# A first slot taken whole, two pairs' exponentials set by set, cheaper means, and a new order: an attention and MLP kernel on one core

## The chip, the cores and the metric

The kernel runs on one core of one Trainium2 chip. The metric is the device time of one execution in microseconds, and lower is better. Times of before: the median of three runs is 711.76 us (711.76 to 712.01).

## What is computed

The reference chains three parts over 2304 tokens of 512 features: an attention with masks, a gated MLP behind an RMS norm, and a second MLP whose activation is a softmax times its own input, with a layer norm behind it.

```python
# attention: B, H, S, D = 4, 8, 576, 64; 4 heads plain window 32, 4 heads dilated by 4
scores = scale * np.matmul(q, k.transpose(0, 1, 3, 2))
scores = np.where(masks[None, :, :, :], scores, -1000000000.0)
scores = scores - np.max(scores, axis=-1, keepdims=True)
attn = np.exp(scores)
attn = attn / (np.sum(attn, axis=-1, keepdims=True) + 1e-09)
out = np.matmul(attn, v)
# MLP: d_model 512, d_ff 1536
rms = np.sqrt(np.mean(x * x, axis=-1, keepdims=True) + 1e-06)
xn = x / rms * rms_g
g = xn @ w_gate
silu = g * (1.0 / (1.0 + np.exp(-g)))
x = silu * (xn @ w_val) @ w_out
# second MLP: d_ff 1024
h = x @ w_in
e = np.exp(h - h_max)
solu = h * e / (np.sum(e, axis=-1, keepdims=True) + 1e-09)
ln = (solu - mu) / np.sqrt(var + 1e-06) * g_ln
out = ln @ w_out
```

The weights arrive in 64-bit floating point, and the kernel makes 32-bit words of them itself.

## The kernel before

**Tiling.** The tokens are cut into nine pieces of 256 (`PIECES`). Pieces 0 and 1 are the early ones: their attention is done by `pair`, with two pairs of heads (t, 0) and (t, 1) each, at the start, while the inputs are still being loaded. Pieces 2 to 8 are done by `attention` later, in between the products of the MLP. The MLP works on parts of one or two pieces (`PARTS`): pieces 0 and 1 are part 0, with 512 columns of tokens. Its hidden dimension is cut into twelve slots f of 128. One slot has a gate product `g`, a value product `vp` (each against four blocks of 128 of the features), then tanh on ScalarE (`u`), the rest of the silu on VectorE (`u<-u,g`), the product with `vp` (`u<-u,vp`), and `y`, which is summed over all slots in four banks. Every product is done as three fp32r matmuls: high with high, low with high and high with low (L952 to L954), so each operand has a high part (a cast on ScalarE, `xh`, `uh`, `w`) and a low part (the rest, on VectorE or GpSimd, `xl`, `uh<-u,uh`, `w<-wf,w`).

**Weights.** `prepare` brings in a slot's three blocks, 0 for the gate, 1 for the values, 2 for y: `fetch` (a load on SyncE's queue of 512 KB, `raw<-w`), `shifted` (ScalarE, on the upper words), `parts` (VectorE, a right shift, L391), `joined` (VectorE, L395, `wf<-raw`), then high and low.

**Norm.** `rms` takes for the early pieces the mean by small `ms<-ones,sq` matmuls, a root on GpSimd (`r`), a diagonal matrix (`rd<-ident,r`, two of 128x128, VectorE, L858), and a `spread` matmul (`rs<-rd,ones`, L863), which puts it on all partitions. For the later pieces the mean comes from one fp32 matmul of 256 columns against `ones` (`ms<-sq,ones`, L827).

**Slot 0.** For part 0 the first slot is done in two halves, piece 0 and piece 1 (`HALVES = 1` and the first two rows of `VIRTUAL`): each half has a gate and a value product of 256 columns, a tanh, a silu, a product and a y of its own.

**Order.** Nothing in the code fixes the order of an engine's instructions by hand. Each piece of work is a step of `Plan`: a name, its cost by engine, the steps that it needs, the buffers that it takes (one bank is named `g`, two are named `vp` and `a`, and so on), and a due time. `order` takes step by step what can start first, and of those that can, the one due first. The table `NUDGE` shifts the due times of single steps, `ENGINE` forces an engine, `PACE` says from which slot on a later attention may begin. So a change to these tables moves instructions on all engines, and each engine then runs its list strictly in that order. Where the plan foresees a gap of TensorE ahead of 75 us (`FILL`), `fill` puts in matmuls on a constant `seed` whose result is overwritten. They are written into the bank that the next step uses:

```python
    def fill(x, add=False):
        while filling[0] > 0:
            filling[0] -= 1
            nc.tensor.matmul(x, (nothing if add else seed)[:, 0:1].to_broadcast([P, P]),
                             seed.to_broadcast([P, x.shape[1]]), start=not add, stop=not add)
```

The third block of work, the joint part for two later parts and the second MLP, is not touched but for its order and its plan costs.

Of the kernel before, what the change touches and what calls it, by code (L numbers as in the profile page):

```python
# [7 lines left out]
F32 = mybir.dt.float32  # L8
# [12 lines left out]
P = 128  # L21
# [4 lines left out]
TP = 256  # L26
# [18 lines left out]
def groups_of(piece):  # L45
# [30 lines left out]
    else:  # L76
# [7 lines left out]
        for at, bt in ((128, b), (192, b2)):  # L84
# [12 lines left out]
HALVES = 1  # L97
# [5 lines left out]
SINGLE = 7  # L103
# [85 lines left out]
class Plan:  # L189
# [20 lines left out]
    def order(self):  # L210
# [32 lines left out]
        while ready:  # L243
# [13 lines left out]
            if e == "p" and free["d"] > start:  # L257
                free["d"] += 0.45 * cost
# [27 lines left out]
def tile_attention_glu_solu(ctx: ExitStack, tc: tile.TileContext, qk_d, v_d, w1_d, win2_d, wout2_d,  # L286
# [24 lines left out]
    ones = const.tile([P, P], F32, name="ones")  # L311
    mhalf = const.tile([P, 4], F32, name="mhalf")
# [45 lines left out]
    def prepare(stage, f, cuts, srcs, scales, dues, needs=(), lead=((1, 0), "joined", 0)):  # L358
# [104 lines left out]
    def pair(t, m, due):  # L463
# [29 lines left out]
        def scores(e):  # L493
            x = new_bank(sp, [P, 8, 64], "sp")
            fill(x.rearrange("p s k -> p (s k)"))
            n = g["mask"]
# [28 lines left out]
        def exps(e):  # L525
            nc.scalar.activation(T[s_], T[sp], AF.Exp, scale=0.125)
# [1329 lines left out]
    for v in range(len(VIRTUAL)):  # L1856
        mlp(v, 1000 * (v + 1))
# [99 lines left out]
```

## Time and profile before

| | before |
|---|---|
| median of three runs | 711.76 us (711.76 to 712.01) |
| the profiled execution | 712.27 us |
| its span | 710.2 us |
| TensorE busy | 702.3 us, 99% |
| VectorE busy | 509.4 us, 72% |
| ScalarE busy | 358.9 us, 51% |
| GpSimd busy | 135.5 us, 19% |
| mean rate of the transfers | 137 GB/s |

The span runs from the first to the last instruction of the profiled execution; the rest of its time lies around it. Engines: PE is TensorE, DVE VectorE, ACT ScalarE, POOL GpSimd, SP SyncE, which issues the loads here. Matmuls are pipelined: the duration of one is longer than the step from one to the next. What a stretch can gain depends on what TensorE waits for there, not on how busy another engine is on average.

### The profile page before, as it was taken

Reading aid. Unit: us, or ns where it says so; the run is one execution under the profiler, and the core shown is the slowest. Engines: PE = TensorE matmul, PEld = TensorE weight load, DVE = VectorE, ACT = ScalarE, POOL = GpSimd, SP = SyncE. Lnnn points to the kernel's source line nnn. Section 1 sums busy time; section 2 is a strip of 40 time slices with the busy share of each in tenths; the row PEclk is TensorE's granted clock in tenths of the full one; section 3 lists DMA queues with packets and bytes.
Section 4 is the critical chain, followed back from the end, with each engine's and each line's share of the span. In section 5 each row is a group of like instructions: output and inputs, shape, how many; then the busy total and the mean of one; then the engine's idle time right before and its main releaser. Section 6 shows DMA issues by size and latency. Waiting matters only on the chain.

```text
span 710.2 us, 11738 instructions
## 1 busy us (share of the span) xinstructions
PE 702.3 (99%) x4533; PEld 593.3 (84%) x4533; DVE 509.4 (72%) x932; ACT 358.9 (51%) x769; POOL 135.5 (19%) x166
## 2 busy tenths in 40 slices
PE   8999999999999999999999999999999999999998
PEld 6788888899998888888888888888888888888887
DVE  5899899679585986668966766689677677665552
ACT  2976854344535554516655554355375555543440
POOL 0322432250506121110000000014044311010110
PEclk9999999999999999999999999999999999999999
DMA  9999433154368764403321112947032111000001
GB/s 336 401 407 354 133 101 118 64 185 141 134 225 293 276 206 141 141 7 125 123 72 37 52 60 97 344 139 220 1 119 75 60 60 45 30 16 30 30 30 45
DMA packets 42424, 97.21 MB, mean 137 GB/s; under 512 B 3841, under 2 KB 14081, under 8 KB 42369
## 3 DMA queue, kind: packets, MB, share of 16 engines
q1 hardware_dynamic: 40640, 93.33, 37.9%
q10 hardware_dynamic: 1728, 3.15, 1.2%
q8 instruction: 35, 0.57, 0.3%
q14 instruction: 21, 0.16, 0.1%
HBM read 72.87 MB, written 23.59 MB: 136 GB/s over the span
## 4 chain that ended last, share of the span: by engine, by line
PE 93%; DMA 5%; ACT 1%; DVE 1%; SPq 0%; issue 0%; ACTq 0%
PE y L952 7%; PE ca L1292 7%; PE y L954 7%; PE y L953 7%; PE o L1689 5%; PE o L1688 5%; PE o L1687 5%; PE g L952 4%; PE vp L952 4%; PE g L953 4%; PE g L954 4%; PE vp L954 4%; PE vp L953 4%; DMA raw<-w 3%; PE cd L1292 2%; PE cb L1292 2%
## 5 line engine op out<-in xcount | busy, mean ns | idle before, releaser
L342 POOL TENSOR_TENSOR w<-wf,w 128x512 fp32r<-128x512 f32 (+1 forms) x15 | 25.1, 1673 | 203.9 <-ACT w L333 203.9
L1687 PE MATMUL o<-w,lt 128*128 128x512 f32 (+1 forms) x152 | 58.9, 388 | 0.0
L1689 PE MATMUL o<-w,lt 128*128 128x512 f32 (+1 forms) x152 | 57.6, 379 | 0.0
L1688 PE MATMUL o<-w,lt 128*128 128x512 f32 (+1 forms) x152 | 57.5, 379 | 0.0
L952 PE MATMUL y<-uh,w 128*128 128x512 f32 (+1 forms) x148 | 53.2, 359 | 0.0
L954 PE MATMUL y<-uh,w 128*128 128x512 f32 (+1 forms) x148 | 51.7, 349 | 0.0
L953 PE MATMUL y<-uh,w 128*128 128x512 f32 (+1 forms) x148 | 51.7, 349 | 0.0
L660 ACT ACTIVATE s<-s,nm 128x64 f32<-128x64 f32 x120 | 40.1, 337 | 18.6 <-DVE nm L655 18.6
L333 ACT CAST w<-wf 128x512 fp32r<-128x512 f32 (+1 forms) x40 | 28.3, 728 | 25.5 <-DVE wf L395 11.5
L952 PE MATMUL g<-xh,w 128*128 128x512 f32 (+1 forms) x104 | 40.4, 389 | 0.0
L333 ACT CAST uh<-u 128x512 fp32r<-128x512 f32 (+1 forms) x37 | 19.9, 537 | 38.3 <-DVE u L996 37.7
L953 PE MATMUL g<-xl,w 128*128 128x512 f32 (+1 forms) x104 | 39.0, 375 | 0.2 <-DVE xl L342 0.2
L952 PE MATMUL vp<-xh,w 128*128 128x512 f32 (+1 forms) x100 | 39.0, 390 | 0.0
L954 PE MATMUL g<-xh,w 128*128 128x512 f32 (+1 forms) x104 | 38.9, 374 | 0.0
L954 PE MATMUL vp<-xh,w 128*128 128x512 f32 (+1 forms) x100 | 38.2, 382 | 0.0
L953 PE MATMUL vp<-xl,w 128*128 128x512 f32 (+1 forms) x100 | 38.1, 381 | 0.0
L805 POOL TENSOR_TENSOR sq<-x 128x256 f32<-128x256 f32 x28 | 17.8, 647 | 105.7 <-DVE x L337 61.6
L1655 POOL TENSOR_SCALAR st<-st 128x1 f32<-128x1 f32 x18 | 8.7, 484 | 140.5 <-ACT sq L1646 140.3
L992 DVE SCALAR_TENSOR_TENSOR u<-u,g 128x512 f32<-128x512 f32 (+1 forms) x37 | 21.5, 582 | 18.3 <-ACT u L986 18.3
L986 ACT ACTIVATE u<-g 128x512 f32<-128x512 f32 (+1 forms) x37 | 19.0, 514 | 27.9 <-PE g L954 27.2
L1689 PEld LDWEIGHTS o<-w,lt 128*128 128x128 f32 x152 | 28.6, 188 | 5.3
L342 DVE TENSOR_TENSOR lt<-tp,lt 128x512 fp32r<-128x512 f32 x36 | 23.2, 684 | 13.6 <-ACT lt L333 13.6
(290 smaller groups left out, 2056.5 us busy)
## 6 DMA issues: line engine op xcount, KB each, us to landing
raw<-w SPq DMA_DIRECT2D x36, 512.0 KB, 9.1
es<-ec SPq DMA_DIRECT2D x12, 512.0 KB, 3.1
sc<-es SPq DMA_DIRECT2D x12, 512.0 KB, 3.4
qk<-qk SPq DMA_DIRECT2D x7, 800.0 KB, 5.5
vt<-v SPq DMA_DIRECT2D x10, 512.0 KB, 5.6
wo<-w SPq DMA_DIRECT2D x9, 512.0 KB, 7.6
wst<-wo SPq DMA_DIRECT2D x9, 512.0 KB, 3.7
yT<-yo SPq DMA_DIRECT2D x16, 256.0 KB, 3.1
```

The source lines that it names most:

```text
L333: nc.scalar.copy(dst, src) if scale is None else nc.scalar.mul(dst, src, scale)
L342: ENG[e].tensor_tensor(dst, a, b, ALU.subtract)
L660: nc.scalar.activation(T[s_][:, i], T[s_][:, i], AF.Exp, bias=st["nm"][:, i:i + 1], accum_out=sm[:, i:i + 1])
L952: nc.tensor.matmul(acc, wh, xh, start=first, stop=False)
L953: nc.tensor.matmul(acc, wh, xl, start=False, stop=False)
L954: nc.tensor.matmul(acc, wl, xh, start=False, stop=last)
L986: return lambda e: nc.scalar.activation(new(up, ("u", v, f), [P, 512])[:, 0:n], T["g", v, f], AF.Tanh, scale=0.5)
L992: return lambda e: nc.vector.scalar_tensor_tensor(out=u_of(f), in0=u_of(f), scalar=1.0, in1=T["g", v, f], op0=ALU.add, op1=ALU.mult)
L1292: nc.tensor.matmul(acc(x), w, y, start=not more and j == 0 and n == 0, stop=j == 1 and n == 2, skip_group_check=True)
L1687: nc.tensor.matmul(o, lt[:, 0, k], w[:, 0], start=(k == 0), stop=False)
L1688: nc.tensor.matmul(o, lt[:, 0, k], w[:, 1], start=False, stop=False)
L1689: nc.tensor.matmul(o, lt[:, 1, k], w[:, 0], start=False, stop=(k == NF2 - 1))
```

## The change

1. Slot 0 of part 0 is no longer in halves. Its gate and value products are still done by piece, but into one bank of 512 columns, with one tanh, silu, product, and one `y` of 512 columns.
2. The pairs (0, 0) and (1, 0) take their exponentials in eight instructions of 64 columns on ScalarE, with the negative maximum as bias and the sums as accumulators (`BY_SET`). The subtraction of the maximum (on VectorE or, for one, on TensorE) and the sum on VectorE go.
3. The blocks of slots 2 to 6 are prepared as blocks 0 and 1 together and block 2 apart (`cuts`). Before, they were all apart.
4. The mean of the pieces from 2 on is taken by two fp32r matmuls over a high and a low part of the squares, which two new steps, `sumhigh` and `sumlow`, make.
5. The diagonal of the early pieces goes to ScalarE by the table `ENGINE`, and so do other steps to other engines; `NUDGE`, `PACE` and the plan costs have many new numbers.
6. Adding the mask to the early scores is a step of its own.

```diff
-HALVES = 1
+BY_SET = ((0, 0), (1, 0))
...
-SINGLE = 7
+APART, WIDE = 2, 7
+
+
+def cuts(f):
+    return [(0,), (1,), (2,)] if f < APART else [(0, 1), (2,)] if f < WIDE else [(0, 1, 2)]
...
+         (('wout', 3), 'fetch'): -31, (('wout', 4), 'fetch'): -39, ((1, 0), 'fetch', 0): -171,
...
+ENGINE = {('copy', (2, 0)): 'd', ('copy', (3, 0)): 'd', ('copy', (5, 0)): 'd', ('copy', (7, 0)): 'd',
+          ('copy', (7, 1)): 'd', ('copy', (8, 1)): 'a', ('diag', 0): 'a', ('diag', 1): 'a', ('ecomb', 0): 'p',
...
-VIRTUAL = [(0, 0, 256, range(HALVES)), (0, 256, 256, range(HALVES)), (0, 0, 512, range(HALVES, NF1)),
-           (1, 0, 256, range(NF1)), (2, 0, 512, range(NF1))]
+VIRTUAL = {2: (0, 0, 512, range(NF1)), 3: (1, 0, 256, range(NF1)), 4: (2, 0, 512, range(NF1))}
...
         def exps(e):
-            nc.scalar.activation(T[s_], T[sp], AF.Exp, scale=0.125)
+            if K not in BY_SET:
+                nc.scalar.activation(T[s_], T[sp], AF.Exp, scale=0.125)
+                return
+            new(stg, s_, [P, 8, 64], name="s")
+            nc.scalar.mul(st["nm"], st["nm"], 0.125)
+            sm = small("sm")
+            for i in range(8):
+                nc.scalar.activation(T[s_][:, i], T[sp][:, i], AF.Exp, scale=0.125, bias=st["nm"][:, i:i + 1], accum_out=sm[:, i:i + 1])
...
         def mean(e):
             x = bank(a_mean, [P, TP], "ms")
-            nc.tensor.matmul(x, ones, T["sq", t, ks[0]], start=True, stop=True)
+            for h in range(2):
+                nc.tensor.matmul(x, ones_r, T["sqh" if h == 0 else "sql", t], start=h == 0, stop=h == 1)
...
-                nc.vector.tensor_scalar(rd[:, P * c:P * c + P], ident, st["r"][:, c:c + 1], None, ALU.mult)
+                put(e, rd[:, P * c:P * c + P], ident, st["r"][:, c:c + 1])
...
+                    fill(T[key][:, 0:TP])
+                else:
+                    filling[0] = 3 * filling[0] // 4
+                    if v == 2 and filling[0] > 0:
+                        fill(psy.tile([P, 512], F32, tag="y00", name="warm")[:, 0:TP])
```

What the tables do to the order is seen at three places. First TensorE, where slot 0 ends and slot 1 begins. In before, behind the last value product of the second half, the first half's y follows, and behind its twelve matmuls slot 1's gate product (`w_0_617` is the gate block of slot 1):

```order
L954 MATMUL vp<-xh,w_1_448 128x256
L952 MATMUL y_620<-uh,w_2_532 128x256
L953 MATMUL y_620<-uh,w_2_532 128x256
L954 MATMUL y_620<-uh,w_2_532 128x256
L952 MATMUL y_624<-uh,w_2_532 128x256
```

In after six fillers into the `g` bank stand there (the last of them is shown), and then slot 1's gate product at once (`w_0_609`):

```order
L1006 MATMUL vp<-xh,w_1_478 128x256
L379 LDWEIGHTS seed
L379 MATMUL g<-seed 128x256
...
L1004 MATMUL g<-xh,w_0_609 128x512
L1005 MATMUL g<-xl,w_0_609 128x512
L1006 MATMUL g<-xh,w_0_609 128x512
```

The y of slot 0 has moved behind slot 1's products, and the fillers write the bank from which VectorE reads slot 0's g.

Second VectorE, around the silu of slot 0. In before (L992 is the silu, L996 the product with the values, L391 and L395 the weights' right shift and join):

```order
L879 SCALAR_TENSOR_TENSOR x<-x,rmsg,rs 128x256 x4
L992 SCALAR_TENSOR_TENSOR u<-u,g 128x256
L342 TENSOR_TENSOR xl<-x,xh 128x2x256 x2
L996 SCALAR_TENSOR_TENSOR u<-u,vp 128x256
L391 TENSOR_SCALAR raw_0_493<-raw_0_493 128x512
L395 SCALAR_TENSOR_TENSOR wf<-raw_0_493 128x512
L342 TENSOR_TENSOR uh<-u,uh 128x256
L992 SCALAR_TENSOR_TENSOR u<-u,g 128x256
```

In after (L1041 is the silu, L1045 the product, L419 and L423 shift and join; `raw_0_502` and `raw_1_399` belong to slot 1, `raw_0_323` with 1024 columns is blocks 0 and 1 of slot 2):

```order
L370 TENSOR_TENSOR xl<-x,xh 128x2x256 x2
L419 TENSOR_SCALAR raw_0_502<-raw_0_502 128x512
L423 SCALAR_TENSOR_TENSOR wf<-raw_0_502 128x512
L423 SCALAR_TENSOR_TENSOR wf<-raw_1_399 128x512
L419 TENSOR_SCALAR raw_0_323<-raw_0_323 128x1024
L1041 SCALAR_TENSOR_TENSOR u<-u,g 128x512
L1045 SCALAR_TENSOR_TENSOR u<-u,vp 128x512
L423 SCALAR_TENSOR_TENSOR wf<-raw_0_323 128x1024
```

There is one silu in place of two, and it stands behind slot 2's right shift.

Third SyncE's queue at the start (`raw` are weight blocks). In before:

```order
L486 DMA qkv<-qk 128x2x800
L1839 DMA masks<-mask 128x704
L486 DMA qkv<-qk 128x2x800
L1839 DMA ident<-ident 128x128
L486 DMA qkv<-qk 128x2x896
L486 DMA qkv<-qk 128x2x800
L490 DMA qkv<-v 128x2x512 x2
L371 DMA raw_0_244<-w 128x1024
```

In after:

```order
L399 DMA raw_0_116<-w 128x1024
L514 DMA qkv<-qk 128x2x800
L1894 DMA masks<-mask 128x704
L514 DMA qkv<-qk 128x2x800
L1894 DMA ident<-ident 128x128
L514 DMA qkv<-qk 128x2x896
L514 DMA qkv<-qk 128x2x800
L518 DMA qkv<-v 128x2x512 x3
```

Slot 0's gate block has moved from behind two v loads to the head of the queue. The last block of slot 2's first two, `raw_0_323` for the second time, is the 26th row of after's queue.

## Rows read from the trace of the kernel before

**Rows 1.** The page: engines, and the chain that ended last, by engine.

```profile
PE 702.3 (99%) x4533; PEld 593.3 (84%) x4533; DVE 509.4 (72%) x932; ACT 358.9 (51%) x769; POOL 135.5 (19%) x166
...
PE 93%; DMA 5%; ACT 1%; DVE 1%; SPq 0%; issue 0%; ACTq 0%
```

**Rows 2.** Waits of TensorE, two of eight: us in total, times, longest.

```profile
PE pv L566 <- DMA qkv<-v: 1.3, 1, 1.3
...
PE tp L675 <- DVE s L668: 0.5, 1, 0.5
...
```

**Rows 3.** Time line of TensorE, 16 to 57 us: start, us, form.

```profile
16.67 1.15 PE L566 MATMUL pv<-xp,qkv 128*64 128x64 f32 x32 [1.25 <-DMA qkv<-v]
...
30.06 1.96 PE L351 MATMUL rs<-seed 128*128 128x256 bf16 x16
32.48 0.70 PE L863 MATMUL rs<-rd,ones 128*128 128x256 f32 x2 [0.46 <-DVE rd L858]
...
39.52 0.28 PE L952 MATMUL y<-uh,w 128*128 128x256 f32 x1
39.64 0.28 PE L953 MATMUL y<-uh,w 128*128 128x256 f32 x1
...
47.89 0.39 PE L952 MATMUL g<-xh,w 128*128 128x512 f32 x1
...
48.34 0.39 PE L954 MATMUL g<-xh,w 128*128 128x512 f32 x1
```

**Rows 4.** Windows: length, PE PEld DVE ACT POOL busy, clock, DMA share, GB/s.

```profile
4.00:17.00 13.00, 11.21 (x179) 8.16 (x178) 8.37 (x16) 3.12 (x5) 0.00 (x0) 1.00 1.04 393
...
45.00:60.00 15.00, 15.00 (x69) 12.44 (x68) 14.01 (x22) 9.07 (x16) 5.66 (x4) 1.00 1.03 407
```

**Rows 5.** SyncE's time line; loads issued at 0.73 and 32.55: KB, us to landing.

```profile
0.73 0.46 SPq L486 DMA_DIRECT2D qkv<-qk  x1
...
32.18 0.80 SPq L371 DMA_DIRECT2D raw<-w  x2
...
qkv<-qk SPq DMA_DIRECT2D x1, 800.0 KB, 4.8
...
raw<-w SPq DMA_DIRECT2D x1, 512.0 KB, 6.0
```

**Rows 6.** VectorE, instructions by form: busy time, mean ns of one, idle before.

```profile
L992 DVE SCALAR_TENSOR_TENSOR u<-u,g 128x512 f32<-128x512 f32 x23 | 15.7, 683 | 11.9 <-ACT u L986 11.9
...
L391 DVE TENSOR_SCALAR raw<-raw 128x512 uint32<-128x512 uint32 x21 | 8.4, 423 | 0.4 <-DMA raw<-w 0.3
...
L391 DVE TENSOR_SCALAR raw<-raw 128x1536 uint32<-128x1536 uint32 x5 | 5.3, 1063 | 0.0
```

**Rows 7.** ScalarE by form: the later pieces' Exp, a copy of 128x128.

```profile
L660 ACT ACTIVATE s<-s,nm 128x64 f32<-128x64 f32 x120 | 40.1, 337 | 18.6 <-DVE nm L655 18.6
...
L333 ACT COPY x<-pv 128x128 f32<-128x128 f32 x4 | 1.3, 434 | 0.0
```

**Rows 8.** Time lines of VectorE and, with POOL, of GpSimd.

```profile
30.85 1.57 DVE L858 TENSOR_SCALAR rd<-ident,r 128x128 f32<-128x128 f32 x2 [0.25 <-POOL r L853]
...
44.00 0.69 DVE L395 SCALAR_TENSOR_TENSOR wf<-raw 128x512 uint32<-128x512 uint32 x1
...
46.00 1.66 DVE L395 SCALAR_TENSOR_TENSOR wf<-raw 128x512 uint32<-128x512 uint32 x1
...
30.87 1.28 POOL L342 TENSOR_TENSOR xl<-xp,xh 128x512 fp32r<-128x512 f32 x1
...
45.72 1.38 POOL L342 TENSOR_TENSOR w<-wf,w 128x512 fp32r<-128x512 f32 x1 [2.99 <-ACT w L333]
```

**Rows 9.** Time line around a mean, 107 to 109 us; then the tile `ms`.

```profile
107.65 0.59 PE L827 MATMUL ms<-sq,ones 128*128 128x256 f32 x2
...
108.31 0.39 PE L953 MATMUL g<-xl,w 128*128 128x512 f32 x1
...
L827 PE MATMUL ms<-sq,ones x14: 377/377/382, 107.6 to 309.3; 128*128 128x256 f32 x14
```

More of the change, by code (lines that the diff above doesn't have):

```diff
@@ L257, in order @@
             if e == "p" and free["d"] > start:
-                free["d"] += 0.45 * cost
+                free["d"] += (0.45 if any(str(x).endswith(("low", "lows")) for x in name) else 0.12) * cost
             done[name] = (e, start + cost)
@@ L495, in scores, with masked @@
             fill(x.rearrange("p s k -> p (s k)"))
+            for y in range(2):
+                for i in range(4):
+                    for c in range(2):
+                        b = 4 * (i // 2) + 2 * c + i % 2
+                        k0 = 512 + g["offs"][b]
+                        nc.tensor.matmul(x[64 * c:64 * c + 64, 4 * y + i, :], qk()[:, y, 64 * b:64 * b + 64],
+                                         qk()[:, y, k0:k0 + 64], start=y == 0 and i == 0, stop=False)
+        def masked(e):
+            x = T[sp]
             n = g["mask"]
@@ L758, in attention @@
             needs_, takes_, uses_ = for_values(K)
-            plan.add(step("values"), {"t": 0.27 + 0.465 * N}, values, needs_, takes=takes_, uses=uses_, due=due)
-        cost = 0.7 if N == 2 and g["kind"] != "tail" else 0.5 * N
-        plan.add(step("copy"), {"d": cost, "a": cost}, copy,
+            plan.add(step("values"), {"t": 0.2 + 0.485 * N}, values, needs_, takes=takes_, uses=uses_, due=due)
+        a, d = (0.62, 0.7) if g["kind"] == "plain" else (0.85, 1.05) if N == 2 else (0.65, 0.6)
+        plan.add(step("copy"), {"d": d, "a": a}, copy,
                  [step("values") if K not in LEADS else ("scores", LEADS[K])] + ([("copy", (t, 0))] if m else []) +
@@ L903, in rms @@
         for k in ks:
[L904 removed]
+            plan.add(step("square", k), {"a": 0.42} if stays else {"a": 0.42, "d": 0.42, "p": 0.75} if first else {"p": 0.64},
                      square(k), [("values", (t, source[k] // 2))] if stays else
@@ L1041, in mlp @@
                         before = [("g", v, f, 1)]
-                    if part == 0 and i == 0 and (f > fs[0] or v in (1, 2)):
-                        before = [("vp", v, f - 1, 1) if f > fs[0] else ("vp", v - 1, HALVES - 1, 1)]
-                    alone = v == 4 and f == 0 and part == 0
-                    plan.add(name, {"t": cost}, by_piece(part, f, (key, v, f), i) if alone else into(part, f, (key, v, f), ks),
-                             before + [made[1, f, part]] + ([(x, k, pieces[i]) for x in ("high", "low") for k in range(2)] if alone else
+                    if part == 0 and i == 0 and f > fs[0]:
+                        before = [("vp", v, f - 1, 1)]
+                    alone = f == 0 and (v == 2 or v == 4 and part == 0)
+                    if alone and part == 1:
+                        before = [("g", v, f, i)] + ([(key, v, f, 0)] if i else [])
+                    plan.add(name, {"t": 1.44 if alone else cost}, by_piece(part, f, (key, v, f), i) if alone else into(part, f, (key, v, f), ks),
+                             before + [made[1, f, part]] + ([(x, k, pieces[i]) for x in ("high", "low") for k in range(2)] if alone and part == 0 else [] if alone else
                                                             ready[i] if f == fs[0] and part == 0 else []),
@@ L1855, in tile_attention_glu_solu @@
                 ([("low", k, 0) for k in range(2)] + [("values", K) for K in EARLY] if f == X_AT else []))
-    for v in range(len(VIRTUAL)):
+    for v in VIRTUAL:
         mlp(v, 1000 * (v + 1))
```

201 lines of the change are left out of this document (108 added, 93 removed), and 6 rows, old and new, of the table ENGINE.

## The prediction, made before the changed kernel ran

> **What bounds the kernel now.** I read the page first. TensorE is busy for 702.3 of 710.2 us, and the chain that ended last is TensorE for 93% [rows 1]. Then the waits of TensorE: eight entries from 1.3 us down, and on a time line only one of them, 0.5 us at a `tp` of the later attention, lies behind 37 us [rows 2]. So from about 37 us to the end the time is the sum of what TensorE issues, and an edit there counts by its matmuls alone, as long as its operands stay early. Ahead of 37 us it is the other way round: there TensorE is fed by the load, and the planner has padded its gaps with filler matmuls on `seed` (sixteen at 30.06 alone [rows 3]), so less work on TensorE is worth nothing there, and what counts is when the slot-0 products end. In before that is at 39.52, where the first `y` starts [rows 3]. From here on I call this moment the end of the front.
>
> The profiled execution took 712.27 for a span of 710.2, so 2.07 us lie outside the span; the median is 711.76, 0.51 below the profiled run. I sum in differences and subtract from the median.
>
> **The change, part by part.**
>
> *The end of slot 0, the largest term.* In after both pieces' gate products go into one bank of 512 columns, and one tanh, one `silu` and one product follow. The order of TensorE shows vp, then six fillers into that same `g` bank, then slot 1's gate product. A filler that writes the bank cannot start until VectorE's `silu` has read slot 0's g from it. And on VectorE the `silu` (L1041) stands behind L419 on `raw_0_323`, 128x1024, the first two weight blocks of slot 2. That instruction waits for a load. So the question is when this load lands.
>
> SyncE's queue gives it. From 4 to 60 us the transfers run at 393 to 407 GB/s, with the DMA share at its full mark and TensorE's granted clock at 1.00 [rows 4]; a block of 512 KB then takes about 1.3 us, and the landing is set by the bytes queued ahead, not by the moment of issue: a weight block issued at 32.55 needed 6.0 us to land [rows 5]. The load in question is the 26th of SyncE's rows in after. The first 26 rows of before are of the same kinds and bytes (four qk, four v, masks, identity, rmsg, fifteen weight blocks), and before's 26th is the second of the pair at 32.18, each of which takes SyncE some 0.4, thus issued at 32.55 and landed at 38.55 [rows 5]. I take 38.55 for after as well.
>
> From there: 0.05 us to be seen, `parts` of 128x1024 (between 0.42 for 512 columns and 1.06 for 1536 [rows 6], so 0.74), the `silu` 0.68 [rows 6], 0.05 to be seen: 40.0. Six fillers at 0.115 (sixteen last 1.96 with a tail of 0.27, so (1.96 − 0.27)/15 [rows 3]) are 0.7, and they cover nothing, since they come after the wait. Slot 1's gate product starts at **40.7**.
>
> *When would TensorE be ready for it?* The front is shorter by the PE work and the DVE subtractions that go, but the weight block now ahead of everything on SyncE's queue takes its 1.3 us from the first qk load (0.73 + 4.8 = 5.53 in before [rows 5], 6.8 in after). I follow it on: the first pv waited for v until 16.67 in before [rows 3], about 17.9 after. The two pairs taken set by set make ScalarE longer (eight Exp of 64 columns at 0.337, 2.7 us [rows 7]) and save VectorE a sum and a subtraction each, for one of them TensorE in its place a matmul, all under these waits. What is late there by 1.2 is won back by the work that goes, and I put the first `spread` 0.2 later than in before. The second gains: in before its operand `rd` took VectorE 1.57 beside a GpSimd `xl` of 1.28, from 30.85 on [rows 8]; ScalarE now makes it, and its nearest row, a 128x128 copy of 0.43 [rows 7], bounds the two between 0.43 and 0.87; by 0.6 the second spread comes at 31.5 in place of 32.48 [rows 3]. Behind it stand, in after, one filler, 24 products of 256 columns at 0.12 (39.52 to 39.64 [rows 3]), five fillers, and 24 more products: 0.5 + 2.87 + 0.6 + 2.87, the end of the front at 38.4. TensorE then waits about 1.5 us, until 40.0. So the end of the front is not what decides; the load is. A front late by another 1.5 us would cost nothing.
>
> In sum, where before's TensorE went on at 39.52, after's goes on at 40.7: **+1.18**.
>
> *The y of slot 0.* 24 matmuls of 256 columns (0.12 each) become 12 of 512 (0.227, the step from 47.89 to 48.34 [rows 3]): 2.87 to 2.72, **−0.15**. The gate and value products keep their forms and counts.
>
> *The means.* Seven pieces have one fp32 `ones` matmul of 256 columns, recorded twice each (14 records [rows 9]). Between 107.65 and 108.31 one of them and one 512-column product lie [rows 9]: 0.66 − 0.227 = 0.433 us for a mean. Its replacement is two fp32r matmuls of 256 columns, 2 × 0.12 = 0.24. No row shows an fp32r matmul on a `ones` weight; the products of 256 columns in this kernel are the nearest, so I take 0.24. Bounds: 0 saved if fp32r here costs as much as fp32, 0.19 each as taken. Seven: **−1.36**. The new `sumhigh` on ScalarE and `sumlow` on VectorE or GpSimd lengthen the norm's chain. They are instructions of 256 columns, between nothing and 0.68 each by the silu of 512 [rows 6], so at most some 1.4 us, in stretches where no `ms` waits at all; I take them at nothing, since TensorE has products of the MLP in its list ahead of the mean.
>
> *Cuts.* Blocks 0 and 1 of slots 2 to 6 are now treated together: fewer, longer instructions of the same columns on ScalarE, VectorE and GpSimd. They cost TensorE nothing as long as the weights come in time. By hand, the low part of slot 3's gate is ready near 55.0 for a product that wants it at 56.8, slot 1's y-weight near 51.7 for 54.1: 1.8 and 2.4 us of cover. VectorE is busy 14.01 of 15 us there already [rows 4], so this cover is what a rival can use up.
>
> *The tables.* The order of nearly everything behind 60 us moves, but TensorE's counts by form are those of before, apart from the terms above, and a saturated TensorE does not feel in which order it works. The one late wait, 0.5 at `tp` [rows 2], may go or be replaced: ±0.5, taken at 0.
>
> Sum: +1.18 − 0.15 − 1.36 = −0.33 us. 712.27 gives 711.9 for a profiled run, and the median 711.76 gives **711.4**.
>
> [...] What VectorE loses beside GpSimd is in rows: a weight join of 512 took 0.69 at 44.00 and 1.66 at 46.00, beside a GpSimd low of 1.38 from 45.72 on [rows 8]; the loss is 0.97. [...]
>
> **Rivals.**
> 1. *The silu is not held* (the load lands over 1 us earlier than summed, since the order on the queue favours it, or VectorE reaches `silu` first). Then TensorE goes on at the end of the front plus `silu` and fillers, 39.1 to 39.6, and the terms are −0.4 to 0.1, −0.15 and −1.36: −1.4 to −1.9, 709.8 to 710.4. For it: one place in the queue is worth 1.3 us by the rate [rows 4], so one place would do most of it. Against: the same bytes stand ahead. Chance 0.12.
> 2. *VectorE falls behind between 45 and 60 us.* It starts slot 1 late, already, with parts and joins of two blocks in its in-order queue, GpSimd lows of 1024 columns beside them (by 1.38 for 512, about 2.6), and a weight low late by over 1.8 us stops TensorE at slot 3's gate. It decides from two slowed instructions on (2 × 0.97). I price it at two more such collisions and one load waited for, +2: 713.4 to 713.9, slower. Chance 0.20.
> 3. *The means are no cheaper.* An fp32r matmul on `ones` costs as its fp32 form does: −1.36 falls away, 712.8. Against: the fp32r products at 0.12 for 256 columns. Chance 0.10.
> 4. My forecast, 0.58: 710.9 to 711.9.
>
> **How the numbers follow.** Runs of this kernel agree within 0.04%, and about 0.2%, 1.42 us, is what a measurement can tell from no change: faster is below 710.34, slower above 713.18. Rival 1 lies at the edge of faster; all of its chance, 0.12, goes there. Rivals 3 and 4 lie within: 0.68. Rival 2 is slower: 0.20. The range of eight in ten leaves out half of rival 1's width below 710.0 and the far half of rival 2: 710.0 to 713.4.
>
> **What would show it.** In after's profile: TensorE's wait list has one of about 1.5 us at a `seed` filler of the `g` bank, released by VectorE `u`, near 38.5 to 40.0; VectorE shows L419 128x1024 ended by a DMA at about 38.6 with `u` right behind it; slot 1's gate at 40.7; two `ms` records of 0.12 pitch for each mean; no TensorE wait over 0.5 behind 41. I am wrong if the load of `raw_0_323` lands elsewhere than at 38.5 ± 0.5, if waits on `w` low stand between 45 and 60 us, or if a mean's neighbours still lie 0.66 apart.

## The result: slower by 1.4%

The changed kernel takes 722.41 us at the median (721.72 to 722.8, four runs), the kernel before 711.88 (711.76 to 712.84, four runs); the ratio is 1.0144, 95% interval 1.0126 to 1.0161. The profiled execution took 722.8.

The page of the changed kernel first: the span, each engine's busy time, and the chain that ended last by engine.

```profile
span 721.0 us, 11743 instructions
...
PE 706.4 (98%) x4536; PEld 594.8 (82%) x4536; DVE 517.3 (72%) x931; ACT 367.2 (51%) x801; POOL 130.3 (18%) x149
...
PE 83%; DVE 8%; DMA 6%; ACT 2%; issue 1%; POOL 0%; SPq 0%; ACTq 0%; DVEq 0%
```

Beside [rows 1], TensorE's share of the chain has fallen from 93% to 83%, and VectorE has 8% where it had 1%. TensorE is busy 4.1 us longer in a span that is 10.8 us longer, so 6.7 us of the loss are idle time and 4.1 us are slower or added work. The waits of TensorE in the changed kernel (us in total, times, longest):

```profile
PE tp L716 <- DVE s L709: 3.8, 2, 3.6
PE tp L716 <- ACT w L361: 1.5, 1, 1.5
PE g L379 <- DVE u L1041: 1.3, 1, 1.3
PE g L1004 <- DVE u L1041: 1.1, 1, 1.1
...
PE ms L869 <- DVE sql L370: 0.7, 1, 0.7
```

The two of 1.1 and 1.3 us at `g` are a late one and the forecast one at the fillers; those at `tp` and `ms` stand far behind 37 us, where before had one wait of 0.5 [rows 2]. On a time line the list runs: 1.3 at 41 us, 1.1 at 85, 1.5 at 104, 3.6 at 124, 0.7 at 238 (`ms`). Now stretches of the changed kernel: length, busy time of PE, PEld, DVE, ACT and POOL, granted clock, DMA share and GB/s.

```profile
78.00:128.00 50.00, 43.60 (x299) 34.79 (x298) 47.71 (x45) 24.15 (x56) 27.22 (x13) 0.97 0.33 110
...
30.00:33.00 3.00, 3.00 (x15) 2.20 (x14) 1.80 (x4) 2.21 (x5) 2.44 (x2) 0.50 1.03 412
120.00:124.00 4.00, 0.42 (x2) 0.00 (x0) 4.00 (x3) 0.60 (x1) 3.36 (x1) 1.00 0.35 131
125.00:128.50 3.50, 3.50 (x10) 2.79 (x9) 1.95 (x5) 0.99 (x2) 0.00 (x0) 0.53 0.00 0
```

From 78 to 128 us TensorE works 43.6 of 50 us, VectorE 47.7. TensorE stands nearly all of 120 to 124, and right behind this its granted clock is 0.53 from 125.0 to 128.5 us; from 30 to 33 us it was 0.50. What holds VectorE is read from its time line and GpSimd's over the same stretch, VectorE first:

```profile
80.31 4.26 DVE L419 TENSOR_SCALAR raw<-raw 128x1536 uint32<-128x1536 uint32 x1
...
91.53 3.50 DVE L419 TENSOR_SCALAR raw<-raw 128x512 uint32<-128x512 uint32 x1
...
104.11 0.95 DVE L419 TENSOR_SCALAR raw<-raw 128x1536 uint32<-128x1536 uint32 x1
104.98 0.67 DVE L1045 SCALAR_TENSOR_TENSOR u<-u,vp 128x512 f32<-128x512 f32 x1
105.57 4.45 DVE L423 SCALAR_TENSOR_TENSOR wf<-raw 128x1536 uint32<-128x1536 uint32 x1
...
111.86 4.87 DVE L423 SCALAR_TENSOR_TENSOR wf<-raw 128x1536 uint32<-128x1536 uint32 x1
...
120.00 3.91 DVE L709 TENSOR_TENSOR s<-s,rn 128x512 f32<-128x512 f32 x1
```

```profile
77.06 6.69 POOL L370 TENSOR_TENSOR w<-wf,w 128x1024 fp32r<-128x1024 f32 x2 [2.52 <-ACT w L361]
91.25 3.48 POOL L370 TENSOR_TENSOR w<-wf,w 128x1536 fp32r<-128x1536 f32 x1 [7.50 <-ACT w L361]
...
104.14 4.27 POOL L370 TENSOR_TENSOR w<-wf,w 128x1536 fp32r<-128x1536 f32 x1
111.62 3.50 POOL L370 TENSOR_TENSOR w<-wf,w 128x1536 fp32r<-128x1536 f32 x1 [3.21 <-ACT w L361]
...
119.49 3.87 POOL L370 TENSOR_TENSOR w<-wf,w 128x1536 fp32r<-128x1536 f32 x1
```

Take them in pairs; "alone" is what the same instruction takes elsewhere in these traces with no GpSimd low beside it. The right shift at 80.31 (1536 columns, 0.95 alone) ends at 84.57, 0.82 behind the end of GpSimd's pair of lows (77.06 + 6.69 = 83.75; the second of the pair has 1536 columns, 3.96 from 79.79 on). The shift at 91.53 (0.42 alone) ends 0.30 behind GpSimd's 94.73. The joins at 105.57 and 111.86 (1.75 alone) end 1.61 behind GpSimd's 108.41 and 115.12, and the product of the softmax weights at 120.00 (0.69 alone), for which TensorE's `tp` waits 3.6 us, ends 0.55 behind 123.36. Each stood until GpSimd's instruction was over and then ran its own time, to within 0.15 us (0.82 for 0.95, 0.30 for 0.42, 1.61 for 1.75, 0.55 for 0.69). It goes the other way too: the shift at 104.11 got in 0.03 ahead of GpSimd's low and kept its 0.95, and that low took 4.27 in place of 3.5. And one of them is not held at all: the product with `vp` at 104.98, which reads a matmul bank, took its usual 0.67 while that low was running.

Where these long lows are from is in GpSimd's instructions by form:

```profile
L370 POOL TENSOR_TENSOR w<-wf,w 128x1536 fp32r<-128x1536 f32 x5 | 19.1, 3819 | 10.7 <-ACT w L361 10.7
...
L370 POOL TENSOR_TENSOR w<-wf,w 128x512 fp32r<-128x512 f32 x6 | 9.2, 1541 | 23.6 <-ACT w L361 23.6
...
L370 POOL TENSOR_TENSOR w<-wf,w 128x1024 fp32r<-128x1024 f32 x3 | 7.6, 2531 | 10.6 <-ACT w L361 10.6
```

Before had fourteen weight lows of 512 columns and one of 1536 on GpSimd; the changed kernel has six of 512, three of 1024 (the joined blocks) and five of 1536, 7.6 and 19.1 us in all.

### The profile page after: what moved, and what is told of

The parts are those of the page before. It is cut to its first block, busy times and chain, and to the rows that moved or that the text cites. A ratio compares the mean times of both kernels' runs of the same rounds, so it can differ in the third digit from the quotient of the medians.

```text
span 721.0 us, 11743 instructions
## 1 busy us (share of the span) xinstructions
PE 706.4 (98%) x4536; PEld 594.8 (82%) x4536; DVE 517.3 (72%) x931; ACT 367.2 (51%) x801; POOL 130.3 (18%) x149
## 4 chain that ended last, share of the span: by engine, by line
PE 83%; DVE 8%; DMA 6%; ACT 2%; issue 1%; POOL 0%; SPq 0%; ACTq 0%; DVEq 0%
PE ca L1347 7%; PE y L1004 6%; PE y L1005 6%; PE y L1006 6%; PE o L1744 5%; PE o L1743 5%; PE o L1742 5%; DMA raw<-w 4%; PE vp L1004 3%; PE vp L1006 3%; PE g L1004 3%; PE vp L1005 3%; DVE wf L423 3%; PE g L1006 3%; PE g L1005 3%; PE cd L1347 2%
## 5 line engine op out<-in xcount | busy, mean ns | idle before, releaser
L1004 PE MATMUL y<-uh,w 128*128 128x512 f32 (+1 forms) x144 | 52.2, 363 | 0.0
L1006 PE MATMUL y<-uh,w 128*128 128x512 f32 (+1 forms) x144 | 51.0, 354 | 0.0
L1005 PE MATMUL y<-uh,w 128*128 128x512 f32 (+1 forms) x144 | 51.0, 354 | 0.0
L370 POOL TENSOR_TENSOR w<-wf,w 128x512 fp32r<-128x512 f32 (+2 forms) x14 | 35.8, 2566 | 44.9 <-ACT w L361 44.9
L361 ACT CAST w<-wf 128x512 fp32r<-128x512 f32 (+2 forms) x35 | 28.0, 806 | 29.1 <-DVE wf L423 17.2
L1005 PE MATMUL vp<-xl,w 128*128 128x512 f32 (+1 forms) x100 | 38.6, 386 | 0.0
L1744 PEld LDWEIGHTS o<-w,lt 128*128 128x128 f32 x152 | 28.6, 188 | 5.3
L370 POOL TENSOR_TENSOR wf<-wf 128x512 f32<-128x512 f32 x2 | 2.8, 1406 | 166.0 <-DVE w L370 153.2
L1743 PEld LDWEIGHTS o<-w,lt 128*128 128x128 f32 x152 | 28.7, 189 | 4.8
```

Of the source, the lines that this page charges most:

```text
L361: nc.scalar.copy(dst, src) if scale is None else nc.scalar.mul(dst, src, scale)
L370: ENG[e].tensor_tensor(dst, a, b, ALU.subtract)
L1004: nc.tensor.matmul(acc, wh, xh, start=first, stop=False)
L1005: nc.tensor.matmul(acc, wh, xl, start=False, stop=False)
L1006: nc.tensor.matmul(acc, wl, xh, start=False, stop=last)
L1743: nc.tensor.matmul(o, lt[:, 0, k], w[:, 1], start=False, stop=False)
```

## Experiments

In all experiments from e1 to e7 the changed kernel keeps its order on every engine but for the instructions named, since the edit stands behind the planner, and likewise in b2 to b5 for the kernel before. Only b1 is planned anew. The changed kernel has three wide lows of 1024 and five of 1536 columns, not four and four as e2's expectation counts them.

**e1: the wide lows in pieces.**

```diff
-                less(e, th[:, :, 1], wf_(c), th[:, :, 0])
+                if e == "p":
+                    for i in range(len(c)):
+                        less(e, th[:, i:i + 1, 1], wf_(c)[:, i:i + 1], th[:, i:i + 1, 0])
+                else:
+                    less(e, th[:, :, 1], wf_(c), th[:, :, 0])
```

> The changed kernel, with GpSimd's weight lows of 1024 and 1536 columns given out as two and three instructions of 512, in the same places; nothing else moves. Theory L (a VectorE instruction that meets a GpSimd low stands until that one instruction ends): no VectorE instruction is held for more than one piece, some 1.3 us, where up to 3.5 were lost; TensorE's waits of 1.1, 1.5 and 3.6 us between 80 and 125 us shrink to under 1 each and the stretch of half clock behind 125 us goes with them: 716, between 714 and 718. Rival W (VectorE has too much work there, whoever it meets): 722, no change.

Measured: 714.78 (714.11 to 715.44), ratio to before 1.0039 (1.0024 to 1.0054); 7.6 us less than the changed kernel. The same joins and the same product on VectorE, then GpSimd's pieces:

```profile
103.62 2.25 DVE L423 SCALAR_TENSOR_TENSOR wf<-raw 128x1536 uint32<-128x1536 uint32 x1
...
108.80 2.78 DVE L423 SCALAR_TENSOR_TENSOR wf<-raw 128x1536 uint32<-128x1536 uint32 x1
...
115.04 1.23 DVE L713 TENSOR_TENSOR s<-s,rn 128x512 f32<-128x512 f32 x1
...
102.18 11.81 POOL L370 TENSOR_TENSOR w<-wf,w 128x512 fp32r<-128x512 f32 x6
```

The joins took 2.25 and 2.78 where they took 4.45 and 4.87, the product 1.23 where it took 3.91, though GpSimd spends more time on its weight lows than in the changed kernel (43.6 us in all in place of 35.9; the six pieces shown 11.8, 1.97 each, where the shortest of before take 1.28 to 1.31). So in this stretch VectorE was held by the length of one GpSimd instruction, not by the amount of work on either engine.

**e2: the wide lows on VectorE.**

```diff
+            if e == "p" and name[1] == "lows" and len(name[0]) == 2 and name[0][0] == 1 and len(cuts(name[0][1])[name[2]]) > 1:
+                e = "d"
             plan.steps[name]["emit"](e)
```

> The changed kernel, with the eight GpSimd weight lows of 1024 and 1536 columns done by VectorE at the same place of the plan. VectorE gets about 4 x 1.2 + 4 x 1.75 = 11.8 us more work of its own before 125 us and is no longer held by these lows. Theory L: what it loses beside them in the trace of the changed kernel is more (some 19 us over seven instructions), so its lists run earlier, TensorE's waits from 80 to 125 us go and the time is 714 to 717. Rival W (too much work on VectorE): waits grow, over 722.

Measured: 713.68 (713.21 to 715.11, ten runs), ratio 1.0027 (1.0018 to 1.0037); 8.7 us less than the changed kernel. Its two longest waits behind 41 us, and the stretch of 78 to 128 us as above:

```profile
PE ms L869 <- DVE sql L370: 1.1, 1, 1.1
...
PE tp L716 <- ACT u L1035: 0.8, 1, 0.8
...
78.00:128.00 50.00, 49.17 (x333) 40.60 (x332) 44.01 (x63) 25.44 (x59) 9.13 (x9) 1.00 0.31 108
```

VectorE has eight instructions more in all (939 for 931) and is busy 44.0 us in this stretch in place of 47.7; TensorE works 49.2 of the 50 us. Rival W is out: with more work of its own VectorE is early.

**e6 and e7: which of the lows.** The edit of e2 for `== 2` (1024 columns) and for `== 3` (1536).

> The changed kernel, with only the three 1024-column weight lows of GpSimd (the blocks that the change joins, slots 2, 4, 6) done by VectorE at the same places. Theory: the costly holds are those of the 1536-column lows at 91 to 124 us, so this takes only the wait of 1.1 us at 85 us and some of the lag: 720 to 721.5. Rival (the joined blocks are what costs): 716 or less.

> The changed kernel, with only the five 1536-column weight lows of GpSimd done by VectorE at the same places. Theory: these hold VectorE for 2.7 to 3.2 us each between 91 and 124 us and make TensorE's waits of 1.5 and 3.6 with the half clock behind: 714.5 to 716.5. Rival (the joined blocks of 1024 are what costs): 720 or more.

Measured: e6 720.40 (719.91 to 721.01), ratio 1.012 (1.0106 to 1.0134), and e7 714.91 (714.22 to 716.11), ratio 1.0044 (1.003 to 1.0058). So 7.5 us hang on the five lows of 1536 columns and 2.0 on the three of 1024; the two add up to 9.5 where e2 gained 8.7, no more apart than the runs of one kernel are. The lows of 1536 are not new as blocks: slots 7 to 11 had joined blocks before as well. It is the tables and the new order that now put five of them on GpSimd in place of one: `ENGINE` names GpSimd for two of the five (slots 7 and 10) and for all three of 1024 columns, and the plan chose it for the rest.

**b3: the same, done to the kernel before.** Its four lows of 1536 columns that VectorE does are given to GpSimd.

```diff
+            if e == "d" and name[1:2] == ("lows",) and name[0][0] == 1 and len(name[0]) == 2 and name[0][1] >= SINGLE:
+                e = "p"
             plan.steps[name]["emit"](e)
```

> The kernel before in its own order, with the four weight lows of 1536 columns that VectorE does between 89 and 116 us (1.75 each) given to GpSimd at the same places, beside the one it has already. VectorE is relieved of 7 us. Theory L: each of GpSimd's 3.5 us holds the VectorE instruction that meets it for up to 3 us, TensorE gets waits of 1 to 3.6 us between 85 and 125 us with half clock behind the longer ones: 715 to 720. Rival W (it is VectorE's amount of work that counts): 711.9, no change.

Measured: 718.61 (716.52 to 720.39), ratio 1.009 (1.0072 to 1.0107). The loss is as expected; the way is partly another. The longest late wait of TensorE, and what GpSimd did ahead of it:

```profile
111.15 0.70 PE L827 MATMUL ms<-sq,ones 128*128 128x256 f32 x2 [2.15 <-POOL sq L811]
...
106.95 3.46 POOL L342 TENSOR_TENSOR w<-wf,w 128x1536 fp32r<-128x1536 f32 x1
110.37 0.72 POOL L811 TENSOR_TENSOR sq<-sq 128x256 f32<-128x256 f32 x1
```

The mean waits for the last add of the squares, which stands on GpSimd behind a low of 3.46. So the long lows cost b3 in two ways: they delay what is queued behind them on GpSimd, and they hold VectorE (`uh` at 118.40 took 3.57 in place of 0.68, beside a low of 3.50 from 117.93 on).

**e3 and e4: the first silu ahead of slot 2's shift,** on the changed kernel (e3) and on e2 (e4).

```diff
+        steps = plan.play()
+        late = next(x for x in steps if x[2] == ((1, 2), "parts", 0))
+        steps.remove(late)
+        steps.insert(next(i for i, x in enumerate(steps) if x[2] == ("silu", 2, 0)) + 1, late)
-        for at_, _, name, e in plan.play():
+        for at_, _, name, e in steps:
```

> The changed kernel, with the right shift of slot 2's blocks 0 and 1 moved behind the first silu on VectorE; nothing else moves. If the shift holds the silu, the silu runs at about 39.1, the wait of 1.3 us at the six fillers goes and slot 1's gate starts near 40.4 in place of 41.7. If that lead lasts, the time is 721.1; if the VectorE chain between 80 and 125 us decides there anyhow, the lead is given back in longer waits and the time stays at 722.4.

> The kernel of e2 (wide lows on VectorE) and also the right shift of slot 2 behind the first silu. With the later waits gone, the lead at slot 1 can last: where the front runs at full clock TensorE's wait for the silu (1.3 to 1.9 us) goes, where it runs at half clock around 30 us (as in e2's profile) TensorE comes late itself and nothing is won. So 712.3 to 713.7, middle 712.9. Rival: the silu's wait is a real cost in every run: 712.2 or less. Rival: no effect at all, 713.7.

Measured: e3 723.14 (720.12 to 724.19), ratio 1.0151 (1.0121 to 1.0181); e4 712.77 (712.13 to 715.11, eleven runs), ratio 1.0022 (1.0012 to 1.0032). In e3 the wait at the fillers is gone and slot 1's gate starts at 40.90 in place of 41.74. The later waits of 1.1, 1.5 and 3.6 us are all there and no longer than they were, and at the last of them the lead is still 0.89 (`tp` at 123.17 in place of 124.06). In the profiled execution it is then lost to the clock: the products behind run at a granted clock of 0.50 from 124.0 to 128.5 us, where the changed kernel's products went from steps of 0.23 us to 0.43 at 125.22, and by 128.7 the two kernels are level; the mean clock of the execution was 0.992, the changed kernel's 0.995. The four runs of e3 lie 4 us apart, so a gain of 0.8 could not have been measured. On e2 the same edit is 0.9 us faster at the median, as expected, with intervals that overlap.

**e5: the mean's own term.** On e2, the two matmuls are replaced by the one fp32 matmul on the sum; the added steps for the high and low part still run, unused.

```diff
-            for h in range(2):
-                nc.tensor.matmul(x, ones_r, T["sqh" if h == 0 else "sql", t], start=h == 0, stop=h == 1)
+            nc.tensor.matmul(x, ones, T["sq", t, ks[0]], start=True, stop=True)
```

> The kernel of e2, with the seven later means taken as before by one fp32 matmul on the sum of squares (the two steps for its high and low part still run, unused; the order stays). The mean's term alone, with TensorE nearly saturated: 0.433 in place of 0.24 each, +1.36: 715.0, between 714.4 and 715.6. Rival (the means cost as much in either form): 713.7.

Measured: 714.87 (714.12 to 716.59), ratio 1.0043 (1.003 to 1.0055), 1.19 above e2, where 1.36 was expected; the two ratios' intervals overlap. The rows do not bear the agreement out. One mean of the seven, first in e2, then in e5:

```profile
228.19 0.28 PE L869 MATMUL ms<-sqh,ones_r 128*128 128x256 f32 x1
229.58 0.39 PE L869 MATMUL ms<-sql,ones_r 128*128 128x256 f32 x1 [1.11 <-DVE sql L370]
```

```profile
229.06 0.59 PE L868 MATMUL ms<-sq,ones 128*128 128x256 f32 x2
229.50 0.60 PE L716 MATMUL tp<-ident,s 128*128 128x128 f32 x4
```

The other six means do take 0.18 to 0.20 more each in e5, 1.14 in all, so the price of a mean is right. But e5 is also rid of e2's wait of 1.1 for `sql`: from this mean to the `tp` behind it e2 needs 1.61 (228.19 to 229.80) and e5 0.44. At the means the two versions come out even, and what makes the measured 1.19 stays open.

**b1, b2 and b4: the means on the kernel before.** b1 has the steps of the changed kernel's means and is planned anew; b2 keeps the order, with the two instructions behind the last add; b4 is b2 with the fp32 mean kept for pieces 3 and 4.

```diff
+            for kind, when in (("sumhigh", done_at), ("sumlow", done_at + 0.5)):
+                while i < mean_at and steps[i][0] <= when:
+                    i += 1
+                steps.insert(i, (steps[i - 1][0], 0, (kind, t), "x"))
+                i, mean_at = i + 1, mean_at + 1
```

> The kernel before, with the two-matmul means of the pieces from 2 on alone (high and low part made by two new steps, planned anew by the same tables). Theory: seven means at 0.24 in place of 0.433 save 1.36 us where TensorE is busy throughout: 710.5, between 709.9 and 711.0. Rival: the two added steps lengthen the norm's chain, or the new order brings a wait, and the gain is lost: 711.9 or more.

> The kernel before in its own order, with the two-matmul means put in by hand: cast and difference of the sum right behind the last add, on ScalarE and VectorE, in buffers that are free there; no other instruction changes place. Theory: b1 lost by its new order, not by the means, so here the term shows: 711.9 - 1.36 = 710.5, between 710.0 and 711.2. Rival: the two added instructions themselves hold something up: 711.9 or more.

> The kernel of b2, with the two-matmul mean for five of the seven pieces and the fp32 mean kept for the two (at 155 and 193 us in the trace of before) at which b2's TensorE had to wait for the added steps. Theory: five times 0.19 saved and no new wait: 712.0 - 0.97 = 711.0, between 710.6 and 711.6. Rival (the added steps cost elsewhere): 712.0 or more.

Measured: b1 720.79 (720.56 to 721.0), ratio 1.0123 (1.0108 to 1.0139); b2 713.49 (713.24 to 716.07), ratio 1.0023 (1.0014 to 1.0032); b4 711.48 (710.81 to 712.31), ratio 0.9993 (0.9984 to 1.0002). b1 missed by 10 us. None of its `ms` matmuls waits; the largest single loss stands behind the last mean (319 us), a wait of TensorE in the joint part (a `ce` matmul), with half clock behind it (windows as above):

```profile
334.79 3.29 PE L1304 MATMUL ce<-w,shl 128*128 128x512 f32 x6 [4.45 <-issue]
...
335.00:338.00 3.00, 2.98 (x7) 1.88 (x8) 3.00 (x5) 1.75 (x4) 0.00 (x0) 0.50 0.33 86
```

So the tables of before, tuned for its own steps, give a time 9 us longer with three steps more, and b1 cannot price the means. b2 missed too: the added steps do hold something up. Its mean at 195 us:

```profile
195.18 0.39 PE L830 MATMUL ms<-sqh,ones_r 128*128 128x256 f32 x1 [1.35 <-ACT sqh L335]
195.64 0.38 PE L830 MATMUL ms<-sql,ones_r 128*128 128x256 f32 x1
```

TensorE waits 1.35 us for the high part, and the matmul on the low part comes 0.46 behind, where 0.12 to 0.2 is the step elsewhere. The cast that makes the high part starts at 194.74, behind the eight Exp of an attention in ScalarE's queue. In the kernel before TensorE did not wait at this mean. b4 leaves out the two means at which b2's matmuls came late (155 and 195 us); its 0.5 us below before is the right sign and half the size, and too little for its interval. A third place is left in it: VectorE stands 2.16 us for the cast of the mean at 255 us, the softmax product behind it comes late, and `tp` waits 0.39 for that, as in b2.

**b5:** b4 with the second early diagonal on ScalarE.

```diff
-                nc.vector.tensor_scalar(rd[:, P * c:P * c + P], ident, st["r"][:, c:c + 1], None, ALU.mult)
+                put("a" if t == 1 else "d", rd[:, P * c:P * c + P], ident, st["r"][:, c:c + 1])
```

> The kernel of b4, with the second early norm's diagonal on ScalarE in place of VectorE (1.57 us beside GpSimd in before, 0.7 on ScalarE in the changed kernel), same place. The second spread comes 0.9 us earlier; the y-weights and the rest of the load bound how much of it lasts: 710.4 to 711.0. Rival (the front is bound by the load): as b4, 711.0.

Measured: 711.61 (711.03 to 712.47), ratio 0.9998 (0.9989 to 1.0007): no gain over b4. That front is bound by the load, as the rival has it, or the gain is below what can be measured. The profiles cannot tell: in both the fillers ran until the second spread at 33.40 (b4) and 33.64 (b5), when the diagonal had long been ready (32.60 and 32.10), and in b4 the granted clock was 0.72 from 28 to 34 us. No version beats the kernel before by a difference that these runs can tell.

## Why the prediction was wrong, step by step

**The tables, taken at 0 ± 0.5, are the step that failed.** That "a saturated TensorE does not feel in which order it works" held only while its operands were early, and I followed the operands only to 60 us. The trace of before shows how little was spare: from 45 to 60 us VectorE was busy 14.01 of 15 us [rows 4]. I had seen that lows were joined and that the tables name an engine for single steps, and did not ask how long GpSimd's instructions become behind 60 us. Eight wide lows, seven of them behind 60 us, cost 8.7 us (e2), and the five of 1536 columns alone 7.5 (e7).

**The price of a collision was too small.** Rival 2 had the mechanism, at 45 to 60 us, with 0.97 a collision and +2 in all. The place was 75 to 125 us, and the holds were 2.7 to 3.3 us each. (Rival 1's own sum is off as well, with nothing hanging on it: 38.4 with the `silu` and the fillers is 39.8, not 39.1 to 39.6.) The prediction took its price from the row of 1.66 [rows 8], where a GpSimd low of 1.38 cost 0.97. Here the lows are 3.48 to 4.27 us long, and in the five pairs shown VectorE stood until the low had ended and then ran its own time, to within 0.15 us; e1, with the lows in pieces, has the same joins at 2.25 and 2.78 in place of 4.45 and 4.87. The row of a neighbour of 1.38 did not bound what one of 3.87 cost: 3.22, for a product of 0.69 alone that took 3.91. The plan's own price is too low as well: it charges VectorE 0.45 of a GpSimd low's planned cost, 1.5 us for 1536 columns (0.25 + 1536/500, times 0.45).

**The cover of the joined blocks** (the step *Cuts*) did last to 60 us, as worked out: the changed kernel has no wait between 42 and 85 us. The three lows of 1024 columns, at 44, 63 and 77 us, cost 2.0 us together: in e6, which moves them, the late wait of 1.1 at 85 us is gone.

**The end of slot 0.** The landing of the load was right. VectorE's shift starts at 38.69, released by the load, where 38.6 was forecast. TensorE, then VectorE and GpSimd, in the changed kernel:

```profile
29.00 3.87 PE L379 MATMUL rs<-seed 128*128 128x256 bf16 x20
32.67 0.79 PE L911 MATMUL rs<-rd,ones 128*128 128x256 f32 x2
...
39.60 0.28 PE L1006 MATMUL vp<-xh,w 128*128 128x256 f32 x1
41.16 0.83 PE L379 MATMUL g<-seed 128*128 128x256 bf16 x6 [1.28 <-DVE u L1041]
41.74 0.47 PE L1004 MATMUL g<-xh,w 128*128 128x512 f32 x1
```

```profile
38.69 1.82 DVE L419 TENSOR_SCALAR raw<-raw 128x1024 uint32<-128x1024 uint32 x1 [0.21 <-DMA raw<-w]
40.44 0.67 DVE L1041 SCALAR_TENSOR_TENSOR u<-u,g 128x512 f32<-128x512 f32 x1
...
38.67 2.98 POOL L370 TENSOR_TENSOR w<-wf,w 128x512 fp32r<-128x512 f32 x2 [5.74 <-ACT w L361]
```

The shift took 1.82 in place of 0.74, beside two GpSimd lows that begin at 38.67, so the silu came at 40.44 (39.3 forecast) and slot 1's gate at 41.74 (40.7 forecast): the term is +2.2 where I had +1.18. (The 0.05 for a result to be seen, which the forecast used without a row, is what lies between the end of the silu, 41.11, and the first filler, 41.16.) TensorE's own readiness was off as well, 39.7 in place of 38.4, since twenty fillers took 3.87 us, most of it at half clock (0.50 from 30 to 33 us), and put the second spread to 32.67. Where the clock stayed up, in e1 (1.00 from 30 to 33 us), the same two lines read:

```profile
29.07 2.40 PE L379 MATMUL rs<-seed 128*128 128x256 bf16 x20
31.64 0.70 PE L915 MATMUL rs<-rd,ones 128*128 128x256 f32 x2 [0.17 <-ACT rd L361]
```

The second spread at 31.64 is the forecast 31.5. What this term is worth in the changed kernel the runs do not settle: e3 takes 0.84 of it away, the lead lasts to 124 us in its trace, and its runs scatter by more than that.

**The y of slot 0 and the means.** A mean costs TensorE 0.24, as taken, where it stands between products (in the changed kernel at 163.00 and 163.12, with the next product at 163.24), and 0.32 behind a `tp` (124.44 to 124.76 below). But "I take them at nothing" for the two added steps was wrong: one `ms` waits 0.7 us in the changed kernel, 1.1 in e2, 1.35 in b2. That takes back between half and all of the 1.36. The term of −0.15 for y was not measured by itself.

```profile
124.06 0.63 PE L716 MATMUL tp<-ident,s 128*128 128x128 f32 x4 [3.64 <-DVE s L709]
124.44 0.36 PE L869 MATMUL ms<-sqh,ones_r 128*128 128x256 f32 x1
124.64 0.28 PE L869 MATMUL ms<-sql,ones_r 128*128 128x256 f32 x1
124.76 0.39 PE L1004 MATMUL vp<-xh,w 128*128 128x512 f32 x1
...
125.64 0.63 PE L1004 MATMUL vp<-xh,w 128*128 128x512 f32 x1
```

**What a wait costs.** These rows show one thing more that the prediction left out. Behind the wait of 3.6 us the products of 512 columns step at 0.43 us in place of 0.23, for some 3.5 us at a granted clock of 0.53. If that is laid to the wait, it cost about 1.7 us a second time (an estimate, 0.47 of 3.5 us).

In sum: e2 brings the changed kernel to 713.7, e4 to 712.8. The 1.4 us that remain to the forecast 711.4 are of the size of e4's wait at `ms` (0.8) and the wait of 0.8 at `tp` that e2 and e4 both show; that they are these was not tried apart.

## What to carry to other kernels

When a table or a planner moves work between VectorE and GpSimd, list GpSimd's instructions by form and look at the longest: here a product that met a low of 3.87 us took 3.91 in place of 0.69, and with the lows cut into pieces of 512 columns the kernel was 7.6 us faster (e1). Where TensorE seems saturated, ask of each producer in its queue how early it is, over the whole stretch that the order changes, and look in the trace for a slow clock behind a long wait (here 3.5 us at 0.53 behind one of 3.6). To price one part of a change under a tuned planner, put it into the fixed order; a new plan (b1) can lose more than any part is worth.

## What the runs showed of the hardware

- In the five pairs shown a VectorE instruction beside a GpSimd low ended 0.30 to 1.61 us behind it, which is the instruction's own time to within 0.15 us: a shift of 0.42 took 3.50 beside a low of 3.48. One low of 1536 columns took 4.27, behind a shift of 0.95 that had begun 0.03 ahead of it, where two others took 3.48 and 3.50. The product with `vp`, which reads a matmul bank, took 0.67 at 104.98 while that low ran, and 0.68 at 103.02 in e1, within the 11.8 us of lows shown there.
- TensorE's granted clock was 0.53 from 125.0 to 128.5 us after 3.6 us of standing, and 0.50 from 335 to 338 us in b1 after 4.45 us. In e1, after 1.85 us, the products of 512 columns stepped at 0.43 us from 42.05 to 44.19, and at 0.23 from 44.52 on. In b3, after 2.15 us, they stepped at 0.23 from 111.92 to 114.23.
- The clock was low around 30 us too in the profiled executions of the changed kernel (0.50 from 30 to 33 us), e2 (0.57), e3 (0.50), e6 (0.57), e7 (0.56) and b4 (0.72 from 28 to 34 us), but 1.00 from 30 to 33 us in those of before, e1, e4, b2 and b3, with nearly the same work ahead; what decides it stays open. In e4 the times part with the mean granted clock: six executions at 0.998 or more took 712.1 to 712.8 us, five at 0.995 took 713.7 to 715.1. In e2 they do not: 713.25 us at 0.995, 715.02 at 0.998.
